# Decoding float64 weights in two VectorE steps, float16 for heads 8 to 15, and channel blocks in parts of 5, 4 and 3

## The chip, the cores and the metric

The kernel runs on one core of one Trainium2 chip. The metric is the time on the device in microseconds, median of the runs. The engines are TensorE (PE: matmuls, PEld: its weight loads), VectorE (DVE), ScalarE (ACT), GpSimd (POOL) and SyncE (SP, whose queue issues the DMAs).

## What is computed

Attention over 4 x 8 heads with a forget gate, then an MLP-mixer block, then a gated convolution block. The sequence has 576 positions, a head 64 columns, the model 512.

```python
scores = q @ k.T / 8 + (cum[:, None] - cum[None, :])   # cum = cumsum(log f), causal mask
attn = softmax(scores); x = attn @ v                    # per head; x is (4, 576, 512)
h = relu(x^T @ w_tok1) @ w_tok2;  u = x + h^T           # 576 -> 256 -> 576
y = u + relu(u @ w_ch1) @ w_ch2                         # 512 -> 1536 -> 512
h = relu(y @ w_in);  c = conv3(h, conv_w)               # 512 -> 1024
out = (h * sigmoid(c)) @ w_out                          # 1024 -> 512
```

The weights of both blocks come as float64. All else is float32.

## The kernel before

**Precision.** A float32 value is held as a high and a low float16 half, and a product is three matmuls, high x high, high x low and low x high (`mm3`, lines 262 to 267). `power_of` (232) finds a power of two from the maximum of a tensor so that the halves fit float16.

**Attention, head by head** (`pair`, `smax`, `sexp`, `pv`). Two heads' scores are made together, in three sets of blocks (lines 862 and 866). VectorE masks them and takes row maxima (880), ScalarE takes the exponential (886). Then the attention matrix is transposed. For heads under `FULL` (16 of 32) TensorE does it in float32, 13 transposes (919), and ScalarE and VectorE copy them out of PSUM (254, 932); PV is one float32 matmul per block (951), 15 blocks. Other heads, except 30 and 31, write a float16 high part on POOL (895) and a low part on VectorE (901), and two DMA transposes from SyncE turn them (911); PV is three float16 matmuls per block (956 to 958). Their V is also split into halves: a sum of absolute values (750), a scale (774), and POOL casts (257, 782). Four heads make a group; a group's token mixing follows it (lines 1059 to 1138, ordered by `group`), and two groups make a batch.

**Channel mixing.** `w_ch1` and `w_ch2` have 12 blocks of 128 hidden columns. They are split into parts (`PARTS_M`). A chunk is half a batch, 288 tokens; there are eight. For a chunk and a part `channel_mix` does 12 matmuls of 288 columns per block, a ReLU on ScalarE (534) and its remainder on VectorE (538), then 12 more per block into four outputs. The first part (`EARLY = 1`) runs beside the attention of later heads, and its results are copied (554) and stored to `p_d`; the others run after the attention and are added to `p` by VectorE (550). `gated` then does the last block, chunk by chunk.

**Weights.** `weight_set` (382) and `weight` (301) load a float64 block as pairs of 32-bit words into one of two buffers `wraw`. ScalarE scales the upper word as a float32 by 2^-112 (406, 328), which moves the exponent. VectorE shifts the result left by three and masks (410), puts the sign in (411), and puts in the top three bits of the lower word (412). A maximum (251) over each block, a spread of it over the partitions by TensorE (245) and `power_of` give the scale; ScalarE and VectorE then make the halves (442, 446). `WT` holds 15 such blocks during the attention.

**Order.** All instructions after the start are issued in an order that `Order` works out when the kernel is built, from a duration, a rank and the dependencies that each task is given (`T(...)`): per engine the task that can start first, then the one of lowest rank. Each engine then runs its list in that fixed order. `SETR` gives the ranks of the early weight sets (of `w_ch1` and of `w_ch2`), `LATER` those of the later parts.

Of the kernel before, what the change touches and what calls it, by code (L numbers as in the profile page):

```python
# [8 lines left out]
F32 = mybir.dt.float32  # L9
F32R = mybir.dt.float32r  # L10
F16 = mybir.dt.float16
I32 = mybir.dt.int32
U8 = mybir.dt.uint8
AF = mybir.ActivationFunctionType
ALU = mybir.AluOpType
# [128 lines left out]
def fox_moe_kernel(  # L144
# [14 lines left out]
    nc = tc.nc  # L159
# [14 lines left out]
    HG = 4  # L174
# [17 lines left out]
    VP_W = 130  # L192
    WSTN = 512

    PARTS_M = (3, 3, 3, 3)
    EARLY = 1
    M_AT = [sum(PARTS_M[:x]) for x in range(len(PARTS_M) + 1)]
    M1 = M_AT[EARLY]
# [2 lines left out]
    NW = 41  # L201
    MM = 0.1226

    FULL = 4 * HG
    BY_PE = [n < FULL or n >= NH - 2 for n in range(NH)]

    SETR = ((0.0, 15.0),)
    LATER = (-10.0, 10.0, 30.0)
    PER = 6.0

    const = ctx.enter_context(tc.tile_pool(name="const", bufs=1))
# [20 lines left out]
    def power_of(dst, ps, n, factor=1.0):  # L232
        nc.vector.tensor_reduce(dst[:, 1:2], ps[:, 0:n], mybir.AxisListType.X, ALU.max)
        nc.vector.tensor_scalar(dst[:, 1:2], dst[:, 1:2], 2.0 ** -60, None, ALU.max)
        up, lo = dst[:, 0:1].bitcast(I32), dst[:, 1:2].bitcast(I32)
        nc.vector.tensor_scalar(up, lo, 0x7F800000, 0x7F800000, ALU.bitwise_xor, ALU.bitwise_and)
        nc.vector.tensor_scalar(lo, lo, 0x7F800000, None, ALU.bitwise_and)
        nc.vector.tensor_scalar(dst[:, 1:2], dst[:, 1:2], 0.5 / factor, None, ALU.mult)
        if factor != 1.0:
            nc.vector.tensor_scalar(dst[:, 0:1], dst[:, 0:1], factor, None, ALU.mult)  # L240

    def spread(stat, n):
        ps = bank("w")[:, 0:128 * n]
# [39 lines left out]
    T = todo.add  # L283
# [12 lines left out]
        return bank(tag)[:, 0, :] if tag == "z" else bank(tag)  # L296


    staged = [0]

    def weight(block, place, rank, key, pools_=(), copy=None):

        src, dims = block
        p = dims[0]
        n = 1
        for d in dims[1:]:
            n *= d
        r = staged[0]
        staged[0] += 1
        box = {}  # L310
        plain = src.dtype == F32

        def shaped(ap):
            return ap.rearrange("p (k n) -> p k n", k=dims[1]) if len(dims) == 3 else ap

        def load():
            if plain:
                box["raw"] = work.tile([128, WSTN, 2], F32, tag="wraw", name="wraw", bufs=2)
                nc.sync.dma_start(shaped(box["raw"].rearrange("p n t -> p (n t)")[0:p, 0:n]), src)
                return  # L320
            box["raw"] = work.tile([128, WSTN, 2], I32, tag="wraw", name="wraw", bufs=2)
            nc.sync.dma_start(shaped(box["raw"][0:p, 0:n, :].rearrange("p n t -> p (n t)")), src.bitcast(I32))

        def exp():
            if plain:
                return
            box["t"] = (cwt if copy else WT[NE - 1 - r % 2])[0:p, 0:n]
            nc.scalar.activation(out=box["t"], in_=box["raw"][0:p, 0:n, 1].bitcast(F32), func=AF.Copy,
                                 scale=2.0 ** -112)

        def dec():
            if plain:
                box["val"] = shaped(box["raw"].rearrange("p n t -> p (n t)")[0:p, 0:n])
                return
            c = box["t"].bitcast(I32)
            nc.vector.tensor_scalar(c, c, 3, 0x7FFFFFF8, ALU.logical_shift_left, ALU.bitwise_and)
            nc.vector.scalar_tensor_tensor(c, box["raw"][0:p, 0:n, 1], -2 ** 31, c, ALU.bitwise_and, ALU.bitwise_or)
            nc.vector.scalar_tensor_tensor(c, box["raw"][0:p, 0:n, 0], 29, c, ALU.logical_shift_right,
                                           ALU.bitwise_or)
            box["val"] = shaped(c.bitcast(F32))  # L340

        def high():
            box["hi"], box["lo"] = place()
            act_cast(box["hi"], box["val"])

        def low():
            pool_sub(box["lo"], box["val"], f32(box["hi"]))

        a, c = ("wraw", r % 2), ("cwt",) if copy else ("W", NE - 1 - r % 2)
        k = n / 512.0  # L350
        T("SP", 0.4, rank - 8, load, writes=[a], moved=0.3 + 1.5 * k * p / 128)
        T("ACT", 0.15 + 0.5 * k, rank, exp, reads=[a], writes=[c])
        T("DVE", 0.2 + 2.4 * k, rank, dec, reads=[a], writes=[c])
        if copy is not None:
            T("DVE", 0.1, rank, lambda: copy(box["val"]), reads=[c], writes=[key])
            return
        T("ACT", 0.15 + 0.5 * k, rank, high, reads=[c], writes=[(key, "h")], pools=pools_)
        T("POOL", 0.1 + 1.3 * k, rank, low, reads=[c, (key, "h")], writes=[key], pools=pools_)
# [7 lines left out]
    WT = {}  # L366
# [15 lines left out]
    def weight_set(name, blocks, raws, first, ranks, cranks, factor):  # L382


        nb = len(blocks)
        stat = const.tile([128, nb], F32, name=f"stat_{name}")
        pw = power(f"pw_{name}")
        box = {}
        for k, (kind, m, (src, dims)) in enumerate(blocks):
            i = raws[k]  # L390
            r = staged[0]
            staged[0] += 1
            plain = src.dtype == F32

            def shaped(ap, dims=dims):
                return ap.rearrange("p (k n) -> p k n", k=dims[1]) if len(dims) == 3 else ap

            def load(k=k, i=i, src=src, plain=plain, shaped=shaped):
                if plain:
                    nc.sync.dma_start(shaped(WT[i]), src)  # L400
                    return
                box[k] = work.tile([128, WSTN, 2], I32, tag="wraw", name="wraw", bufs=2)
                nc.sync.dma_start(shaped(box[k].rearrange("p n t -> p (n t)")), src.bitcast(I32))

            def exp(k=k, i=i):
                nc.scalar.activation(out=WT[i], in_=box[k][:, :, 1].bitcast(F32), func=AF.Copy, scale=2.0 ** -112)

            def dec(k=k, i=i):
                c = WT[i].bitcast(I32)
                nc.vector.tensor_scalar(c, c, 3, 0x7FFFFFF8, ALU.logical_shift_left, ALU.bitwise_and)  # L410
                nc.vector.scalar_tensor_tensor(c, box[k][:, :, 1], -2 ** 31, c, ALU.bitwise_and, ALU.bitwise_or)
                nc.vector.scalar_tensor_tensor(c, box[k][:, :, 0], 29, c, ALU.logical_shift_right, ALU.bitwise_or)

            a = ("wraw", r % 2)
            w = [("W", i)]
            if plain:
                T("SP", 0.4, ranks[k] - 8, load, reads=opened(i), writes=w, moved=1.0)
            else:
                T("SP", 0.4, ranks[k] - 8, load, writes=[a], moved=1.8)
                T("ACT", 0.65, ranks[k], exp, reads=[a, *opened(i)], writes=w)  # L420
                T("DVE", 2.3, ranks[k], dec, reads=[a], writes=w)
            T("DVE", 0.65, ranks[k], lambda k=k, i=i: largest(stat[:, k:k + 1], WT[i]), reads=w,
              writes=[("stat", name, k)])

        def across():
            nc.vector.tensor_reduce(stat[:, 0:1], stat, mybir.AxisListType.X, ALU.max)

        def span():
            box["ps"] = spread(stat, 1)

        kw = turn("w")
        st = [("stat", name, k) for k in range(nb)]
        T("DVE", 0.1, cranks[0], across, reads=st[1:], writes=st[:1])
        T("PE", 0.25, cranks[0], span, reads=st, writes=[kw], ring=[kw])
        T("DVE", 0.7, cranks[0], lambda: power_of(pw, box["ps"], 128, factor), reads=[kw], writes=[("pw", name)], ring=[kw])
        for k, (kind, m, _) in enumerate(blocks):
            i = raws[k]
            j = first if k == 0 else raws[k - 1]
            wslot[kind, m] = j

            def high(i=i, j=j):
                nc.scalar.activation(out=WT[j].bitcast(F16)[:, 0:512], in_=WT[i], func=AF.Copy, scale=pw[:, 0:1])

            def low(i=i, j=j):
                t = WT[j].bitcast(F16)
                nc.vector.scalar_tensor_tensor(t[:, 512:1024], WT[i], pw[:, 0:1], t[:, 0:512], ALU.mult, ALU.subtract)

            T("ACT", 0.75, cranks[k], high, reads=[("W", i), ("pw", name), *opened(j)], writes=[("W", j)])
            T("DVE", 0.75, cranks[k], low, reads=[("W", i), ("pw", name)], writes=[("W", j)])
        return pw  # L450
# [188 lines left out]
    with tc.manual_schedule():  # L639
# [558 lines left out]
        AVAIL = [(H * (b + 1) - 1) * PER + 30 for b in range(B)]  # L1198
        LATE = 1000.0
        for k, (block, hi, lo) in enumerate(tok_w):  # L1200
            weight(block, lambda hi=hi, lo=lo: (hi, lo), 4 + 5.0 * k, ("tokw", k), pools_=["a1"])
        t0 = AVAIL[0] - 30
        at = 0
        for x in range(EARLY):
# [257 lines left out]
```

## Time and profile before

| | |
|---|---|
| median of 3 runs | 751.34 us (750.29 to 753.07) |
| the profiled execution | 751.88 us, span 750.0 us |
| TensorE busy | 732.8 us, 98% |
| VectorE busy | 563.7 us, 75% |
| ScalarE busy | 399.3 us, 53% |
| POOL busy | 182.4 us, 24% |
| mean granted clock of TensorE | 0.991 |

A busy time is the union of the engine's instructions. Matmuls overlap in the pipeline: one of 288 columns is shown with 287 ns, but the next one starts long before it ends. A float32 matmul appears as two records. In a window row, xN is the number of instructions in the window.

### The profile page before, as it was taken

To read this page: it belongs to the slowest core of one execution; us is meant where nothing else is said; L and a number is where in the kernel's file an instruction comes from. 1 tells how busy PE (TensorE), PEld (TensorE's weight loads), DVE (VectorE), ACT (ScalarE), POOL (GpSimd) and SP (SyncE) were. 2 spreads that over 40 slices of the span, in tenths; PEclk is the share of its full clock that TensorE was granted. 3 is DMA by queue.
4 is the path that set the end of the run, shared out by engine and by line. 5 is a ranking of instruction groups with operands and counts; after the bars stand their busy time and mean duration, and the time that the engine had idled before them with its cause. 6 is when DMAs were issued, how large, how long until landed. Compare 5 with 4: busy or idle time off the path is not lost.

```text
span 750.0 us, 16275 instructions
## 1 busy us (share of the span) xinstructions
PE 732.8 (98%) x6396; PEld 600.9 (80%) x6396; DVE 563.7 (75%) x1349; ACT 399.3 (53%) x862; POOL 182.4 (24%) x242
## 2 busy tenths in 40 slices
PE   7999999998999999999999999999999999999997
PEld 5889889887786878878787777778878878778785
DVE  5788899889896778878888886336749767965551
ACT  5875667665575464645324223112248766776663
POOL 2221114173646414000003103011003323323230
PEclk8999999999999999999999999999999999999999
DMA  9454544567898868835348444054111212100101
GB/s 218 148 165 154 153 137 139 185 125 192 180 230 192 162 126 280 260 106 183 128 119 244 144 142 140 2 159 126 33 64 33 64 33 64 48 18 33 34 26 38
DMA packets 126381, 94.31 MB, mean 126 GB/s; under 512 B 64672, under 2 KB 118432, under 8 KB 126304
## 3 DMA queue, kind: packets, MB, share of 16 engines
q1 hardware_dynamic: 126304, 93.27, 44.8%
q8 instruction: 50, 0.82, 0.5%
q14 instruction: 27, 0.22, 0.1%
HBM read 57.73 MB, written 23.59 MB: 108 GB/s over the span
## 4 chain that ended last, share of the span: by engine, by line
PE 81%; DVE 7%; issue 5%; POOL 3%; ACT 3%; DMA 0%; SPq 0%; POOLq 0%; ACTq 0%; DVEq 0%
PE w L265 13%; PE w L266 12%; PE w L267 12%; PE z L266 8%; PE z L265 8%; PE z L267 8%; PE w L951 7%; PE z L862 6%; PE w L919 3%; POOL g L260 2%; DVE pl L901 1%; PE w L1096 1%; PE z L866 1%; DVE t L880 1%; ACT t L886 1%
## 5 line engine op out<-in xcount | busy, mean ns | idle before, releaser
L265 PEld LDWEIGHTS <-w 128*128 128x128 f16 x1280 | 125.4, 98 | 34.5 <-issue 3.0
L267 PEld LDWEIGHTS <-w 128*128 128x128 f16 x1280 | 125.6, 98 | 33.0 <-issue 1.1
L266 PEld LDWEIGHTS <-w 128*128 128x128 f16 x1280 | 125.3, 98 | 33.2 <-issue 2.0
L534 ACT ACTIVATE r<-w 128x288 f16<-128x288 f32 x96 | 39.2, 408 | 129.8 <-PE w L267 128.7
L1362 DVE SCALAR_TENSOR_TENSOR cv<-hp,cw,cv 128x286 f32<-128x286 f32 (+1 forms) x128 | 74.7, 590 | 43.6 <-ACT cv L1356 41.4
L266 PE MATMUL w<-ul,w 128*128 128x288 f16 x352 | 101.1, 287 | 0.0
L265 PE MATMUL w<-uh,w 128*128 128x288 f16 x352 | 101.1, 287 | 0.0
L267 PE MATMUL w<-uh,w 128*128 128x288 f16 x352 | 101.0, 287 | 0.0
L260 POOL TENSOR_TENSOR g<-sg,g 128x286 f16<-128x286 f32 (+1 forms) x64 | 54.5, 858 | 168.1 <-ACT g L254 166.3
L886 ACT ACTIVATE t<-t,m 128x448 f32<-128x448 f32 (+4 forms) x160 | 81.9, 553 | 23.8 <-DVE m L880 23.2
L265 PE MATMUL z<-r,w 128*128 128x288 f16 x288 | 82.3, 286 | 0.4 <-DVE p L550 0.3
L265 PE MATMUL w<-vh,w 128*128 128x288 f16 x288 | 82.4, 286 | 0.0
L266 PE MATMUL w<-vl,w 128*128 128x288 f16 x288 | 82.4, 286 | 0.0
L267 PE MATMUL w<-vh,w 128*128 128x288 f16 x288 | 82.4, 286 | 0.0
L267 PE MATMUL z<-r,w 128*128 128x288 f16 x288 | 82.4, 286 | 0.0
L266 PE MATMUL z<-r,w 128*128 128x288 f16 x288 | 82.4, 286 | 0.0
L880 DVE CUSTOM_DVE_ANT_0 t<-z,mask 64x64 f32<-64x64 f32 (+4 forms) x160 | 70.0, 480 | 10.0 <-PE z L866 9.8
L266 PE MATMUL z<-g,w 128*128 128x286 f16 (+1 forms) x256 | 73.3, 286 | 0.7 <-POOL g L260 0.7
L265 PE MATMUL z<-g,w 128*128 128x286 f16 (+1 forms) x256 | 73.0, 285 | 1.0 <-ACT g L254 1.0
L267 PE MATMUL z<-g,w 128*128 128x286 f16 (+1 forms) x256 | 72.9, 285 | 0.0
L611 POOL TENSOR_TENSOR p<-p,u 128x288 f32<-128x288 f32 x32 | 29.1, 941 | 175.6 <-DMA p<-p_d 86.7
L550 DVE SCALAR_TENSOR_TENSOR p<-z,backs,p 128x288 f32<-128x288 f32 x96 | 48.6, 515 | 29.7 <-PE z L267 25.3
(185 smaller groups left out, 1647.0 us busy)
## 6 DMA issues: line engine op xcount, KB each, us to landing
wraw<-in_moe_w_ch_dram SPq DMA_DIRECT2D x24, 512.0 KB, 3.9
qk<-in_qk_dram SPq DMA_DIRECT2D x16, 608.0 KB, 4.9
u_d<-us SPq DMA_DIRECT2D x8, 576.0 KB, 4.3
p_d<-res SPq DMA_DIRECT2D x32, 144.0 KB, 3.1
p<-p_d SPq DMA_DIRECT2D x8, 576.0 KB, 4.6
u<-u_d SPq DMA_DIRECT2D x8, 576.0 KB, 4.5
x_d<-p SPq DMA_DIRECT2D x8, 576.0 KB, 3.2
u<-x_d SPq DMA_DIRECT2D x8, 576.0 KB, 3.9
```

Source lines behind the costliest of these rows:

```text
L260: nc.gpsimd.tensor_tensor(o, a, b, ALU.subtract)
L265: nc.tensor.matmul(ps, wh, xh, start=(first and i == 0), stop=False)
L266: nc.tensor.matmul(ps, wh, xl, start=False, stop=False)
L267: nc.tensor.matmul(ps, wl, xh, start=False, stop=(last and i == n - 1))
L534: nc.scalar.activation(out=t[:, 0, :], in_=box["z", m], func=AF.Relu)
L550: nc.vector.scalar_tensor_tensor(t, box["o", d], back, t, ALU.mult, ALU.add)
L611: nc.gpsimd.tensor_tensor(box["p"][:, d], box["p"][:, d], box["u"][:, d], ALU.add)
L862: nc.tensor.matmul(out_[x], t[r, Q0[i]:Q0[i] + 128], t[r, k0:k0 + n], start=first, stop=False)
L880: nc.vector.tensor_tensor_reduce(to, z_t.pop((n, i)), mk, -0.125, 3e38, ALU.add, ALU.min, m_t[n][0:rows, i:i + 1])
L886: nc.scalar.activation(out=tt[0:rows, o:o + w], in_=tt[0:rows, o:o + w], func=AF.Exp, bias=m_t[n][0:rows, i:i + 1], scale=-1.0)
L951: nc.tensor.matmul(o[:, 0:65], p32(n)[:, 128 * blk:128 * blk + 128], vp32_t[g % 2][:, slot, hh, :], start=(j == 0), stop=(j == nb - 1))
L1362: nc.vector.scalar_tensor_tensor(cv, hp_t[m][:, s0 + t:s1 + t], cw[:, t, m:m + 1], cv, ALU.mult, ALU.add)
```

## The change

It touches five things.

- `PARTS_M` goes from (3, 3, 3, 3) to (5, 4, 3): the early part has five blocks of twelve, and there are two later parts instead of three. `SETR` and `LATER` give other ranks, and the token weights' rank starts at 10 instead of 4.
- `FULL` goes from 16 to 8 heads: heads 8 to 15 take the float16 path, and groups 2 and 3 have their V split.
- Decoding: ScalarE uses Prelu with the slope -2^32 for negative values, so that the sign lands in a bit that survives the shift. VectorE then takes two steps, a shift of the lower word in its buffer and a shift and OR.
- The scale of a decoded block comes from ScalarE's Square with a sum (`accum_out`), written over the raw buffer, in place of VectorE's maximum. The raw buffer is thus held until Square has run. `power_of_root` makes the power of two from the sum of squares.
- The tasks' durations and dependencies follow.

```diff
-    PARTS_M = (3, 3, 3, 3)
+    PARTS_M = (5, 4, 3)
-    FULL = 4 * HG
+    FULL = 2 * HG
-    SETR = ((0.0, 15.0),)
-    LATER = (-10.0, 10.0, 30.0)
+    SETR = ((-5.0, 30.0),)
+    LATER = (-10.0, 20.0, 40.0)
+    def power_of_root(dst, ps, n, factor):
+        nc.vector.tensor_reduce(dst[:, 1:2], ps[:, 0:n], mybir.AxisListType.X, ALU.max)
+        nc.vector.tensor_scalar(dst[:, 1:2], dst[:, 1:2], 2.0 ** -120, None, ALU.max)
+        up, lo = dst[:, 0:1].bitcast(I32), dst[:, 1:2].bitcast(I32)
+        nc.vector.tensor_scalar(lo, lo, 1, 0x7F800000, ALU.logical_shift_right, ALU.bitwise_and)
+        nc.vector.tensor_scalar(up, lo, 0x7F800000, None, ALU.bitwise_xor)
+        nc.vector.tensor_scalar(dst[:, 1:2], dst[:, 1:2], 2.0 ** 64 / factor, None, ALU.mult)
+        nc.vector.tensor_scalar(dst[:, 0:1], dst[:, 0:1], 2.0 ** -65 * factor, None, ALU.mult)
+    def shifted(o, raw):
+        nc.scalar.activation(out=o, in_=raw[:, :, 1].bitcast(F32), func=AF.Prelu, scale=2.0 ** -112, alpha=-2.0 ** 32)
+    def joined(o, raw):
+        c, low = o.bitcast(I32), raw[:, :, 0]
+        nc.vector.tensor_scalar(low, low, 29, None, ALU.logical_shift_right)
+        nc.vector.scalar_tensor_tensor(c, c, 3, low, ALU.logical_shift_left, ALU.bitwise_or)
             def exp(k=k, i=i):
-                nc.scalar.activation(out=WT[i], in_=box[k][:, :, 1].bitcast(F32), func=AF.Copy, scale=2.0 ** -112)
+                shifted(WT[i], box[k])
             def dec(k=k, i=i):
-                c = WT[i].bitcast(I32)
-                nc.vector.tensor_scalar(c, c, 3, 0x7FFFFFF8, ALU.logical_shift_left, ALU.bitwise_and)
-                nc.vector.scalar_tensor_tensor(c, box[k][:, :, 1], -2 ** 31, c, ALU.bitwise_and, ALU.bitwise_or)
-                nc.vector.scalar_tensor_tensor(c, box[k][:, :, 0], 29, c, ALU.logical_shift_right, ALU.bitwise_or)
+                joined(WT[i], box[k])
+            def squares(k=k, i=i):
+                nc.scalar.activation(out=box[k][:, :, 1].bitcast(F32), in_=WT[i], func=AF.Square,
+                                     accum_out=stat[:, k:k + 1])
-                T("DVE", 2.3, ranks[k], dec, reads=[a], writes=w)
-            T("DVE", 0.65, ranks[k], lambda k=k, i=i: largest(stat[:, k:k + 1], WT[i]), reads=w,
-              writes=[("stat", name, k)])
+                T("DVE", 1.25, ranks[k], dec, reads=w, writes=[a, *w])
+            if plain:
+                T("DVE", 0.65, ranks[k], lambda k=k, i=i: largest(stat[:, k:k + 1], WT[i]), reads=w,
+                  writes=[("stat", name, k)])
+            else:
+                T("ACT", 0.9, ranks[k], squares, reads=w, writes=[a, ("stat", name, k)])
-            weight(block, lambda hi=hi, lo=lo: (hi, lo), 4 + 5.0 * k, ("tokw", k), pools_=["a1"])
+            weight(block, lambda hi=hi, lo=lo: (hi, lo), 10 + 5.0 * k, ("tokw", k), pools_=["a1"])
```

`weight` changes its decode in the same way, with a task of 0.15 + 1.2 per 512 elements in place of 0.2 + 2.4.

## Rows read from the trace of the kernel before

**Rows 1.** The page: busy time, share of the span and instructions of each engine.

```profile
PE 732.8 (98%) x6396; PEld 600.9 (80%) x6396; DVE 563.7 (75%) x1349; ACT 399.3 (53%) x862; POOL 182.4 (24%) x242
```

**Rows 2.** Busy time by stretch: from:to length, engines (instructions), granted clock, DMA share, GB/s.

```profile
10.00:50.00 40.00, 37.98 (x283) 30.95 (x285) 29.24 (x103) 32.24 (x70) 10.20 (x11) 0.93 0.56 159
50.00:90.00 40.00, 40.00 (x334) 36.00 (x335) 34.95 (x94) 25.67 (x57) 4.24 (x5) 1.00 0.55 167
90.00:163.00 73.00, 72.86 (x611) 64.78 (x609) 66.78 (x186) 46.93 (x100) 21.16 (x29) 1.00 0.54 157
163.00:286.00 123.00, 116.49 (x1417) 96.17 (x1414) 102.69 (x282) 73.20 (x155) 56.57 (x57) 0.97 0.78 173
...
375.00:400.00 25.00, 25.00 (x206) 20.03 (x205) 21.50 (x59) 8.15 (x18) 0.00 (x0) 1.00 0.59 144
```

**Rows 3.** Waits of TensorE, 90 to 286 us: total, times, longest in us.

```profile
PE w L245 <- DVE um L251: 2.8, 1, 2.8
```

**Rows 4.** The chain that ended last, in order of time: start, us, what.

```profile
20.17 3.49 PE w L951 x30
...
69.84 1.32 PE w L919 x12
```

**Rows 5.** Timeline: first PV matmul of head 27, and the next other one.

```profile
261.62 0.19 PE L956 MATMUL w<-vp,pt 128*128 128x65 f16 x1
...
263.01 0.28 PE L265 MATMUL w<-r,w 128*128 128x288 f16 x1
```

**Rows 6.** Groups by line and shape: busy us, mean ns, idle time before.

```profile
L550 DVE SCALAR_TENSOR_TENSOR p<-z,backs,p 128x288 f32<-128x288 f32 x96 | 48.6, 515 | 29.7 <-PE z L267 25.3 <-issue 4.0
L538 DVE SCALAR_TENSOR_TENSOR r<-w,r 128x288 f16<-128x288 f32 x96 | 43.4, 453 | 35.2 <-ACT r L534 34.4
...
L411 DVE SCALAR_TENSOR_TENSOR w<-wraw,w 128x512 int32<-128x512 int32 x40 | 30.6, 765 | 1.4
...
L406 ACT ACTIVATE w<-wraw 128x512 f32<-128x512 f32 x40 | 26.7, 672 | 16.2 <-DMA wraw<-in_moe_w_in_dram 6.5 <-DMA wraw<-in_moe_w_out_dram 5.3 <-DMA wraw<-in_moe_w_ch_dram 4.3
...
L901 DVE SCALAR_TENSOR_TENSOR pl<-t,ph 128x1024 f16<-128x1024 f32 x14 | 19.7, 1404 | 1.3 <-POOL ph L895 1.3
L446 DVE SCALAR_TENSOR_TENSOR w<-w,pw_c,w 128x512 f16<-128x512 f32 x24 | 19.1, 794 | 3.0 <-ACT w L442 3.0
...
L410 DVE TENSOR_SCALAR w<-w 128x512 int32<-128x512 int32 x40 | 18.8, 471 | 2.8 <-ACT w L406 2.7
...
L251 DVE TENSOR_REDUCE stat_c<-w 128x1 f32<-128x512 f32 x24 | 16.2, 674 | 0.1
...
L901 DVE SCALAR_TENSOR_TENSOR pl<-t,ph 128x640 f16<-128x640 f32 x14 | 13.8, 983 | 1.9 <-POOL ph L895 1.8
...
L932 DVE COPY pt<-w 128x512 f32<-128x512 f32 x16 | 10.9, 682 | 2.1 <-PE w L919 2.0
```

**Rows 7.** Groups of ScalarE, same columns: load of the table for Exp, accumulator read.

```profile
L886 ACT ACT_TABLE_LOAD x1 | 1.3, 1283 | 0.0
...
L750 ACT ACTIVATION_READ_ACCUMULATOR junk<-vf 128x1 f32 x4 | 0.8, 189 | 0.0
```

**Rows 8.** DMA issues, of a block of weights: KB each, median us to landing.

```profile
wraw<-in_moe_w_ch_dram SPq DMA_DIRECT2D x24, 512.0 KB, 3.9
```

**Rows 9.** The last decoding step (line 412) by stretch: VectorE busy (instructions), clock, DMA.

```profile
50.00:90.00 40.00, 5.93 (x7) 1.00 0.55 167
90.00:163.00 73.00, 5.56 (x7) 1.00 0.54 157
163.00:286.00 123.00, 0.00 (x0) 0.97 0.78 173
```

**Rows 10.** ReLUs (line 534), then result copies (554), of the mix in heads 16 to 31.

```profile
163.00:286.00 123.00, 4.04 (x10) 0.97 0.78 173
...
163.00:286.00 123.00, 5.93 (x12) 0.97 0.78 173
```

**Rows 11.** All ReLUs of the mix (line 534): ns min/median/max, first and last start.

```profile
L534 ACT ACTIVATE r<-w x96: 387/410/411, 119.4 to 550.9; 128x288 f16<-128x288 f32 x96
```

More of the change, by code (lines that the diff above doesn't have):

```diff
@@ L327, in exp @@
             box["t"] = (cwt if copy else WT[NE - 1 - r % 2])[0:p, 0:n]
-            nc.scalar.activation(out=box["t"], in_=box["raw"][0:p, 0:n, 1].bitcast(F32), func=AF.Copy,
-                                 scale=2.0 ** -112)
+            shifted(box["t"], box["raw"][0:p, 0:n])
         def dec():
@@ L334, in dec @@
                 return
-            c = box["t"].bitcast(I32)
-            nc.vector.tensor_scalar(c, c, 3, 0x7FFFFFF8, ALU.logical_shift_left, ALU.bitwise_and)
[L337 to L340, printed above, removed]
+            joined(box["t"], box["raw"][0:p, 0:n])
+            box["val"] = shaped(box["t"])
         def high():
@@ L352, in weight @@
         T("ACT", 0.15 + 0.5 * k, rank, exp, reads=[a], writes=[c])
-        T("DVE", 0.2 + 2.4 * k, rank, dec, reads=[a], writes=[c])
+        T("DVE", 0.15 + 1.2 * k, rank, dec, reads=[c], writes=[a, c])
         if copy is not None:
@@ L388, in weight_set @@
         box = {}
+        bring = power_of if blocks[0][2][0].dtype == F32 else power_of_root
+        if bring is power_of_root:
+            factor *= 4.0
         for k, (kind, m, (src, dims)) in enumerate(blocks):
@@ L405, in exp @@
             def exp(k=k, i=i):
-                nc.scalar.activation(out=WT[i], in_=box[k][:, :, 1].bitcast(F32), func=AF.Copy, scale=2.0 ** -112)
+                shifted(WT[i], box[k])
             def dec(k=k, i=i):
-                c = WT[i].bitcast(I32)
-                nc.vector.tensor_scalar(c, c, 3, 0x7FFFFFF8, ALU.logical_shift_left, ALU.bitwise_and)
-                nc.vector.scalar_tensor_tensor(c, box[k][:, :, 1], -2 ** 31, c, ALU.bitwise_and, ALU.bitwise_or)
-                nc.vector.scalar_tensor_tensor(c, box[k][:, :, 0], 29, c, ALU.logical_shift_right, ALU.bitwise_or)
+                joined(WT[i], box[k])
+            def squares(k=k, i=i):
+                nc.scalar.activation(out=box[k][:, :, 1].bitcast(F32), in_=WT[i], func=AF.Square,
+                                     accum_out=stat[:, k:k + 1])
             a = ("wraw", r % 2)
@@ L434, in weight_set @@
         T("PE", 0.25, cranks[0], span, reads=st, writes=[kw], ring=[kw])
-        T("DVE", 0.7, cranks[0], lambda: power_of(pw, box["ps"], 128, factor), reads=[kw], writes=[("pw", name)], ring=[kw])
+        T("DVE", 0.7, cranks[0], lambda: bring(pw, box["ps"], 128, factor), reads=[kw], writes=[("pw", name)], ring=[kw])
         for k, (kind, m, _) in enumerate(blocks):
```

## The prediction

> **What bounds the kernel now.** I read four views in this order: the page's busy times, the busy time by stretch, the chain that ended last, and the groups by line. The page gives TensorE 98% of the span and VectorE 75% [rows 1]. Busy time of TensorE overlaps, so I check it by counting: in 375 to 400 us it runs 206 matmuls of 288 columns, one each 0.121 us, with no gap [rows 2]. From 310 us on the kernel is that: a queue of channel-mix and output matmuls. Time comes off there only if matmuls go away.
>
> Before 310 us there are three stages. In 10 to 50 us TensorE is idle 2.0 us of 40 by the busy row. In 50 to 163 us (heads 4 to 15) it is idle 0.1 us; here the float32 attention keeps it full, and VectorE is nearly full as well (66.8 of 73 us in 90 to 163) [rows 2]. In 163 to 286 us (heads 16 to 31, float16) TensorE is idle 6.5 us of 123, and its mean granted clock is 0.97 there against 1.00 before, 3% of 123 us, 3.7 us lost [rows 2]. So float16 heads cost 10.2 us of idle and slow time over 16 heads, 0.64 us each; float32 heads cost next to none. One idle stretch there is a wait for VectorE: 2.8 us in a spread of the group's maximum [rows 3].
>
> The profiled execution took 751.88 us with a span of 750.0; the median is 751.34. I sum against 751.9 and take 0.5 off at the end.
>
> **Heads 8 to 15 in float16 (TensorE).** A float32 head does its PV in 30 recorded matmuls, 3.49 us, and 13 transposes at 1.32/12 = 0.11 us, 1.43 us [rows 4]. A float16 head does 45 matmuls for PV: head 27 begins at 261.62 and the next matmul begins at 263.01, so 1.39 us [rows 5], and its transposes go to the DMA. Saved per head: 3.49 + 1.43 - 1.39 = 3.53 us. The chain's 3.49 includes the tail of the last matmul (some 0.13 us of issue), so I take 3.41; eight heads, 27.3 us (28.2 at most). This is TensorE work, in a stage where TensorE had no gap, so it is worth its full size if something fills TensorE afterwards. Two more value sums for groups 2 and 3 cost it under 1 us, and two weight sets less give that back.
>
> **Parts 5, 4, 3.** No matmul is added or removed: two more of twelve blocks for eight chunks, 2 x 24 x 8 = 384 matmuls, 46.5 us at 0.121, move from the late to the early queue. Early ones are what fills TensorE beside the heads. 32 additions on VectorE (one part less, 8 chunks, 4 each, 0.515 us) go away, 16.5 us; they lay beside a TensorE that starts a matmul each 0.121 us, so I cost them at nothing; if VectorE set the pace there they would be worth up to that.
>
> **The decode.** Per weight VectorE ran 471 ns, twice 765 (line 412 is of the same form as 411) and a maximum of 674 [rows 6]. Now it runs one single-source step and one of 0.765. The single-source step reads every second word; its bounds are L410's 471 ns (also single-source, contiguous) and L411's 765 (the same strided buffer, but two sources). I take 471, the row with the same form. So 0.765 + 0.674 = 1.44 us less per weight, 1.14 at least. For the 26 weights decoded after 163 us that is 37 us, again beside a full TensorE: nothing, by the same reason and with the same price if the cover went. The Trainium skill, "VectorE: DVE Perf Modes", section "What auto-detection actually checks", asks unit steps only of 16-bit tensors for a doubled rate, so it would keep the strided step near 0.47; no row of this trace shows a strided single-source step.
>
> ScalarE gets Prelu for Copy at equal size (672 ns for 512 elements) and a Square with an accumulator: I price it as one more such pass plus the accumulator read of 189 ns, 0.86 us [rows 6, 7], at least 0.67. ScalarE is busy 46.9 of 73 us in 90 to 163 [rows 2], so ten of them, 8.6 us, hide in the 26 that are free; without that cover they would cost those 8.6. Square is a new wait of ScalarE for VectorE: the Exps of the next blocks and the evacuations of PSUM queue behind it, and VectorE and TensorE wait for those. What waits behind them: the raw buffer is released by Square instead of by the decode. One turn of a buffer was 3.9 us landing [rows 8] + 0.67 + 2.00 = 6.6 us; it becomes 3.9 + 0.67 + 1.24 + 0.86 = 6.7. The load that queues on SyncE behind it is therefore not later.
>
> **VectorE while heads 8 to 15 run.** Start from 66.8 us [rows 2]. The low parts cost 1.404 + 0.983 and replace a copy of 0.682, eight times: +13.6. Seven decodes fall there [rows 9]: -10.0 (-7.9 at the slow bound). Five low halves more at 0.79: +4.0. Ten remainders of the early mix, one batch, at 0.453: +4.5 [rows 6]. Sum 78.9. TensorE has 73 - 27.3 = 45.7 us of attention there, and one batch of early mix (240 x 0.121 = 29.0): 74.7. So VectorE becomes the longer one: 4.2 us of TensorE idle if VectorE were full, 11.5 if it stays at its present share (78.9/0.915 = 86.2). The 0.64 us per head of the existing float16 heads gives 5.1 for eight. I take 6.5, nearest to that row since it is the same work, and keep 4 and 11.5.
>
> POOL gets eight heads' high parts and the values of two groups; it is busy 21.2 of 73 us there, and 56.6 of 123 where nearly every head has them. SyncE gets sixteen transposes; the DMA share is 0.54 in that stage and 0.78 where nearly every head has them [rows 2]. Neither is last.
>
> **Sum.** 751.9 - 27.3 + 6.5 = 731.1; less 0.5, 730.6. I forecast **731 us**.
>
> **The rivals.** *VectorE relief removes old idle too.* The 10.2 us of idle and slow time in 163 to 286 are queue order and VectorE lateness; more early mix lies ready there (batches 0 and 1 together 58 us; now 10 ReLUs and 12 result copies run there, 10 x 12 + 12 x 9 = 228 matmuls, 28 us [rows 10]), and lighter decoding also helps the start, 2 us idle. If half to all of it went, 5 to 12 us: 719 to 726. Against it: hardly any decode runs in 163 to 286 (none of the third steps [rows 9]), so the relief is elsewhere.
>
> *The fill is smaller than the hole.* VectorE at its present share (11.5), plus a clock of 0.97 over that stage too and two to three waits like the 2.8 us one: idle 13 to 22, so 738 to 747. For it: VectorE at 66.8 of 73 already.
>
> *The gain is eaten.* Idle of 24 to 31: 748 to 755. It needs the same loss in heads 16 to 31 as well.
>
> *The early mix comes too late, slower.* This is the other side. The second half of a mix needs all ten early weights, where six sufficed, and the new ranks put its five weights at 30, behind heads of lower rank. Before, the first ReLU of the early mix ran at 119.4 us [rows 11]. Fourteen weights were decoded by 163 us, seven before 90 [rows 9]; at that pace the tenth is decoded near 121 us and its halves are done near 130, while the first halves can start earlier. If instead the set is ready only after head 15, TensorE has 45.7 us of work in a stage that VectorE paces at 79 to 86: idle 33 to 40, 751.4 - 27.3 + 33..40 = 757 to 764. It turns slower than now beyond 0.5% when idle passes 31 us, that is when fewer than (86 - 45.7 - 31)/0.121, some 75, early-mix matmuls run before head 16.
>
> *Prelu or Square isn't in the table loaded with Exp.* Then a decode between two Exps costs two loads of 1.283 us [rows 7]; 21 decodes in 10 to 163 us make 54 us on a ScalarE that is busy 104.8 of 153 there [rows 2], and with the Squares it would need some 171: 18 us beyond the stage and more in waits, 745 to 765. Against it: Copy, Abs, Relu and Exp alternate now, with one load at the first Exp [rows 7]. The Trainium skill, "ScalarE: Activation LUTs", section "Table sets: the hidden batching unit", names relu, copy, identity and abs as members of every set, and does not name Prelu or Square there; with its figure of about 2.66 us for a switch the 54 us would be an estimated 112.
>
> **How the numbers follow.** About 0.5% (747.6 to 755.1) is what a measurement of this kernel can tell from no change. Forecast, 726 to 738: 0.53. VectorE relief, 717 to 726: 0.21. Smaller fill, 738 to 747: 0.15. Eaten: 0.05. Early mix too late: 0.04. Table loads: 0.02. Faster 0.89, same 0.05, slower 0.06. The range 717 to 745 leaves out the last three and the upper end of the third.
>
> **What would show it.** The PV of heads 8 to 15 at 1.39 us each and only 130 recorded transposes (10 heads); early mix running beside heads 8 to 15; the attention ending near 310 us still, but with far more early mix done by then; seven of twelve blocks left for after it; the saturated stage at 0.121 us as now. The strided step at 0.47 or 0.77 us. One Exp table load. I am wrong if TensorE idles over 20 us more before 310, or if the float16 heads' stage is longer than 86 us for eight heads.

## The result, and the profile after

| | before | after |
|---|---|---|
| median | 751.49 us (750.29 to 753.07, 4 runs) | 728.29 us (725.97 to 730.78, 4 runs) |
| ratio of the medians | | 0.9691 [0.9653, 0.9729] |
| the profiled execution | 751.88 us, span 750.0 | 727.58 us, span 725.8 |
| PE, DVE, ACT, POOL busy | [rows 1] | 706.5, 502.8, 420.8, 214.8 us |

The forecast was 731 us with a range of 717 to 745. Line numbers moved, by 11 in the helpers (`mm3` 276, spread of a maximum 256, maximum 262) and by 23 behind the decoding: scores 885, masks 903, Exp 909, high parts 918, low parts 924, transposes 942, float32 PV 974, float16 PV 979 to 981, early ReLU 557, early copies 577, low halves 469.

Busy time by stretch of the changed kernel, columns as in [rows 2]:

```profile
10.00:50.00 40.00, 38.83 (x296) 32.36 (x298) 25.16 (x94) 31.70 (x71) 10.68 (x15) 0.91 0.60 173
50.00:90.00 40.00, 37.77 (x305) 33.12 (x302) 31.08 (x89) 29.54 (x65) 17.63 (x21) 0.98 0.55 158
90.00:163.00 73.00, 67.34 (x729) 53.58 (x728) 68.92 (x176) 50.48 (x108) 39.78 (x34) 0.94 0.91 204
163.00:286.00 123.00, 121.22 (x1433) 99.98 (x1430) 100.38 (x273) 73.18 (x154) 57.41 (x56) 1.00 0.93 200
...
375.00:400.00 25.00, 25.00 (x206) 20.02 (x205) 18.29 (x48) 14.28 (x33) 0.00 (x0) 1.00 0.46 124
```

Against [rows 2], two stages changed in opposite directions. In 50 to 163 us TensorE was idle for 0.1 us only and had its full clock; now it is idle 2.23 + 5.66 us at a clock of 0.98 and 0.94. In 163 to 286 it was idle 6.5 us at 0.97; now 1.8 at 1.00. The saturated queue at 375 us runs 206 matmuls in 25 us, as before.

Groups by line and shape of the changed kernel: busy us, mean ns of one, idle before.

```profile
L318 DVE SCALAR_TENSOR_TENSOR w<-w,wraw 128x512 int32<-128x512 int32 x42 | 32.5, 773 | 8.1 <-ACT w L313 4.8
...
L313 ACT ACTIVATE w<-wraw 128x512 f32<-128x512 f32 x42 | 27.9, 672 | 4.1 <-DMA wraw<-in_moe_w_out_dram 2.1 <-DMA wraw<-in_moe_w_in_dram 1.3 <-DMA wraw<-in_moe_w_ch_dram 0.6
...
L431 ACT ACTIVATE wraw<-w 128x512 f32<-128x512 f32 x40 | 26.9, 673 | 19.4 <-DVE w L318 18.2 <-DVE rs L989 1.0
...
L317 DVE TENSOR_SCALAR wraw<-wraw 128x512 int32<-128x512 int32 x42 | 20.3, 483 | 1.6 <-DMA wraw<-in_moe_w_in_dram 1.2 <-DMA wraw<-in_moe_w_ch_dram 0.3
...
L942 PE MATMUL w<-ident,t 128*128 128x128 f32 x130 | 17.9, 278 | 0.6 <-DVE pt L963 0.2 <-ACT t L909 0.2 <-DVE xf L998 0.2
...
L431 ACT ACTIVATION_READ_ACCUMULATOR wraw<-w 128x1 f32 x40 | 7.4, 186 | 0.0
...
L909 ACT ACT_TABLE_LOAD x1 | 1.3, 1283 | 0.0
```

The decode is two VectorE steps of 483 and 773 ns, Square costs 0.673 + 0.186 = 0.86 us, 130 transposes are left (10 heads of 13), and the table for Exp is loaded once. The timeline shows the first two of the new float16 heads, the first PV matmul and the first one after them; 2.76 us for both, 1.38 us a head:

```profile
99.66 0.20 PE L979 MATMUL w<-vp,pt 128*128 128x65 f16 x1
...
102.42 0.46 PE L256 MATMUL w<-ident,um 128*128 128x128 f32 x2
```

TensorE's waits of the changed kernel over the whole execution (total, times, longest in us). The wait for the group's maximum is down from 2.8 [rows 3] to 0.8, and those for a mask lead:

```profile
PE z L885 <- DVE m L903: 3.9, 4, 1.8
...
PE w L256 <- DVE um L262: 0.8, 1, 0.8
```

**A balance from the window rows.** Take as time lost by TensorE in a stretch its idle time plus (1 - granted clock) x length, as the prediction did for heads 16 to 31. Then a kernel's span should be 750.0, less the 27.3 us of TensorE work where heads 8 to 15 are float16, plus the difference in lost time. For the thirteen other kernels (below) this gives the measured span within 4.1 us, and for the changed one 727.6 against 725.8. "Chain" is the time that VectorE's decoding steps hold on the chain that ended last (with the old decode the maximum of each block too), added up over its pieces from 10 to 310 us. All times in us, from the profiled execution.

| kernel | span | lost 10-50 | 50-163 | 163-286 | 286-330 | sum | span worked out | chain |
|---|---|---|---|---|---|---|---|---|
| before | 750.0 | 4.8 | 0.1 | 10.2 | 0.0 | 15.1 | | 0 |
| after | 725.8 | 4.8 | 13.1 | 1.8 | 0.4 | 20.0 | 727.6 | 1.7 |
| f16_only | 753.1 | 3.6 | 14.2 | 21.2 | 2.6 | 41.6 | 749.2 | 19.7 |
| decode_only | 754.8 | 5.0 | 2.1 | 12.4 | 0.7 | 20.2 | 755.1 | 5.2 |
| parts_only | 762.1 | 12.7 | 5.2 | 5.3 | 0.4 | 23.6 | 758.5 | 12.0 |
| no_f16 | 741.6 | 5.0 | 0.2 | 3.7 | 0.0 | 8.9 | 743.8 | 0 |
| no_decode | 760.3 | 9.5 | 20.6 | 18.2 | 0.4 | 48.7 | 756.3 | 20.6 |
| no_parts | 749.3 | 4.8 | 16.3 | 16.0 | 5.2 | 42.3 | 749.9 | 7.5 |
| no_join | 726.7 | 4.7 | 14.4 | 1.8 | 0.4 | 21.3 | 728.9 | 0 |
| v_late | 739.1 | 4.4 | 21.0 | 9.6 | 0.4 | 35.4 | 743.0 | 4.0 |
| tok_rank4 | 727.7 | 4.8 | 13.5 | 1.8 | 0.9 | 21.0 | 728.6 | 9.0 |
| true_costs | 738.0 | 2.8 | 18.1 | 9.4 | 0.4 | 30.7 | 738.3 | 2.5 |
| parts66 | 730.9 | 4.6 | 16.7 | 0.1 | 0.6 | 22.0 | 729.6 | 5.5 |
| full12 | 729.1 | 4.0 | 2.7 | 0.6 | 0.7 | 8.0 | 729.3 | 3.0 |

(full12 has half of the 27.3 us. Fixed windows hold slightly different heads in each kernel, and what is lost after 330 us is not in the table. The idle times that some expectations name, 68 and 38 us, 30 us added, 18 us before head 16, are larger than its figures, 41.6, 15.1, 26.5 and 13.1. tok_rank4 is as fast as the changed kernel with 9.0 us of decoding on its chain against 1.7, so time on the chain is not a price by itself.)

### The profile page after: what moved, and what is told of

Read it like the earlier page. It is cut to its first block, busy times and chain, and to the rows that moved or that the text cites. A ratio compares the mean times of both kernels' runs of the same rounds, so it can differ in the third digit from the quotient of the medians.

```text
span 725.8 us, 16282 instructions
## 1 busy us (share of the span) xinstructions
PE 706.5 (97%) x6412; PEld 573.8 (79%) x6412; DVE 502.8 (69%) x1225; ACT 420.8 (58%) x924; POOL 214.8 (30%) x270
## 4 chain that ended last, share of the span: by engine, by line
PE 81%; DVE 7%; issue 6%; POOL 4%; ACT 1%; DMA 0%; SPq 0%; POOLq 0%; DVEq 0%; ACTq 0%
PE w L276 14%; PE w L277 14%; PE w L278 14%; PE z L277 7%; PE z L278 7%; PE z L276 7%; PE z L885 6%; PE w L974 3%; PE w L942 2%; POOL g L271 2%; PE z L889 2%; DVE pl L924 1%; PE w L1119 1%; PE w L980 1%; PE w L979 1%
## 5 line engine op out<-in xcount | busy, mean ns | idle before, releaser
L276 PE MATMUL w<-uh,w 128*128 128x288 f16 x416 | 119.8, 288 | 0.0
L278 PE MATMUL w<-uh,w 128*128 128x288 f16 x416 | 119.6, 288 | 0.0
L277 PE MATMUL w<-ul,w 128*128 128x288 f16 x416 | 119.6, 288 | 0.0
L909 ACT ACTIVATE t<-t,m 128x576 f32<-128x576 f32 (+4 forms) x160 | 81.7, 554 | 20.9 <-DVE m L903 18.5
L903 DVE CUSTOM_DVE_ANT_0 t<-z,mask 128x576 f32<-128x576 f32 (+4 forms) x160 | 70.5, 479 | 17.9 <-PE z L889 17.8
L561 DVE SCALAR_TENSOR_TENSOR r<-w,r 128x288 f16<-128x288 f32 x96 | 43.4, 453 | 43.4 <-ACT r L557 43.2
L885 PE MATMUL z<-qk 64*128 64x288 f32 (+4 forms) x384 | 61.8, 432 | 7.0 <-DVE m L903 3.9
L271 POOL TENSOR_TENSOR xl<-xf,xh 128x320 fp32r<-128x320 f32 x32 | 34.0, 1064 | 110.2 <-ACT xh L265 110.1
L276 PE MATMUL w<-vh,w 128*128 128x288 f16 x224 | 64.1, 286 | 0.0
L277 PE MATMUL w<-vl,w 128*128 128x288 f16 x224 | 64.1, 286 | 0.0
L278 PE MATMUL w<-vh,w 128*128 128x288 f16 x224 | 64.1, 286 | 0.0
L276 PE MATMUL z<-r,w 128*128 128x288 f16 x224 | 64.1, 286 | 0.0
```

Of the source, the lines that this page charges most:

```text
L271: nc.gpsimd.tensor_tensor(o, a, b, ALU.subtract)
L276: nc.tensor.matmul(ps, wh, xh, start=(first and i == 0), stop=False)
L277: nc.tensor.matmul(ps, wh, xl, start=False, stop=False)
L278: nc.tensor.matmul(ps, wl, xh, start=False, stop=(last and i == n - 1))
L561: nc.vector.scalar_tensor_tensor(t[:, 1, :], box["z", m], 0.0, f32(t[:, 0, :]), ALU.max, ALU.subtract)
L885: nc.tensor.matmul(out_[x], t[r, Q0[i]:Q0[i] + 128], t[r, k0:k0 + n], start=first, stop=False)
```

## The experiments

The theories on record: in one (A) the lighter decode on VectorE is what keeps TensorE fed beside the float16 heads; in the other (B) it is the larger early part, with its new ranks. Each of the first six kernels has one or two of the three parts of the change.

**Float16 for heads 8 to 15 alone** (from the kernel before).

```diff
-    FULL = 4 * HG
+    FULL = 2 * HG
```

> The kernel before with only heads 8 to 15 in float16; old decode, parts of 3. If the gain is TensorE work taken away (27.3 us), most of it comes here, less idle: VectorE then has 66.8 + 13.6 = 80.4 us to do beside heads 8 to 15, and TensorE 45.7 us of attention plus 17.4 of early mix, so 17 to 25 us of idle: 741 to 750. If the gain is VectorE's relief by the decode, this is no faster than before: 751 or more. If it is the moved mix, the same.

755.68 us, 1.0064 [1.0045, 1.0084]. The first range is missed: slightly slower than before, the outcome named for a gain by the decode or by the moved mix. TensorE's 27.3 us went, and 26.5 us came back as lost time, 14 in heads 4 to 15 and 11 in heads 16 to 31; another 3.0 us are idle in 330 to 500 us. Heads 16 to 31 of this kernel:

```profile
163.00:286.00 123.00, 109.14 (x1210) 87.75 (x1209) 111.31 (x287) 71.25 (x147) 57.38 (x53) 0.94 0.90 201
```

VectorE is busy 111.3 of 123 us and TensorE idles 13.9. The chain that ended last says with what (start, us, what; L410 to L412 are the old decode, L880 the mask):

```profile
163.66 1.17 DVE w L410
...
164.86 1.03 DVE w L411
...
165.91 2.44 DVE w L412
168.36 0.40 DVE t L880
...
168.81 0.91 ACT t L886 x2
```

One decode holds VectorE for 4.7 us between two masks, and the mask and the Exp wait for it. TensorE has other work until 180 us (no idle time in 160 to 180); then it is idle 3.4 and 3.1 us in the next two stretches of 10 us, waiting for low halves of `u` and for masks, VectorE's work. By the groups' means the decode should take 2.0 us [rows 6]. Its last step took 2.44 us where the median of line 412 in this kernel is 0.692. POOL's timeline in that stretch, and that of the kernel before:

```profile
164.62 3.20 POOL L782 TENSOR_TENSOR vp<-vf,vp 64x256 f16<-64x256 f32 x2
...
165.07 3.86 POOL L782 TENSOR_TENSOR vp<-vf,vp 64x256 f16<-64x256 f32 x3
```

POOL is doing the value split of a later group, and it did the same at that time in the kernel before; the splits of the two added groups ran at 51 and 91 us. What is new beside it is the decode. Line 412 in heads 16 to 31 of this kernel, where the kernel before ran none [rows 9]:

```profile
163.00:286.00 123.00, 7.01 (x6) 0.94 0.90 201
```

Before, fourteen ran in 50 to 163 us; here eight do, and six come later, among VectorE's 111.3 us of work. In all the old decode holds 19.7 us of this kernel's chain, and 0 of the kernel before's.

**The decode alone** (`shifted`, `joined`, Square, `power_of_root` and their tasks; `FULL`, `PARTS_M` and ranks as before).

```diff
-                T("DVE", 2.3, ranks[k], dec, reads=[a], writes=w)
+                T("DVE", 1.25, ranks[k], dec, reads=w, writes=[a, *w])
...
+                T("ACT", 0.9, ranks[k], squares, reads=w, writes=[a, ("stat", name, k)])
```

> The kernel before with only the new decode and the sums of squares. If TensorE's work sets the time, the relief can only remove idle that VectorE causes in heads 16 to 31 and at the start: 746 to 751. If VectorE's relief is the gain: 728 to 738.

756.78 us, 1.0075 [1.0051, 1.0098]. A miss, slightly slower. There is little to gain where TensorE hardly waited: lost time is 20.2 against 15.1, 2.0 more in 50 to 163 us and 2.2 more in heads 16 to 31.

**The parts and ranks alone.**

```diff
-    PARTS_M = (3, 3, 3, 3)
+    PARTS_M = (5, 4, 3)
-    SETR = ((0.0, 15.0),)
-    LATER = (-10.0, 10.0, 30.0)
+    SETR = ((-5.0, 30.0),)
+    LATER = (-10.0, 20.0, 40.0)
```

(and the token weights' rank 10 for 4)

> The kernel before with only parts of 5, 4, 3 and their ranks. TensorE's work is unchanged and it is full beside heads 4 to 15; more early mix can only fill the idle of heads 16 to 31: 747 to 753 if TensorE's work sets the time. If moving the mix is the gain: 730 to 740.

764.29 us, 1.0185 [1.0148, 1.0221]. A miss, and the slowest. Heads 16 to 31 did gain (10.2 lost to 5.3: 14 ReLUs of the mix run there, against 10 in [rows 10]). Most of the loss is at the start, 12.7 for 4.8; 5.1 more are lost in 50 to 163, and TensorE is idle 3.8 us in 330 to 400. The chain at 33 us, where lines 336 to 338 are the old decode in `weight`:

```profile
32.96 0.63 DVE w L336
...
33.62 0.47 DVE w L337
...
34.11 0.44 DVE w L338
...
35.24 0.23 DVE w L336
...
36.92 0.67 DVE t L880
```

Two decodes stand ahead of a mask (the new decode with the same ranks, no_f16, loses 5.0 in this stage), and after the gap TensorE runs at a lower clock, in 30 to 50 us:

```profile
30.00:40.00 10.00, 7.99 (x53) 5.80 (x52) 8.11 (x25) 7.99 (x17) 3.99 (x4) 0.86 0.33 98
40.00:50.00 10.00, 8.95 (x51) 8.15 (x50) 6.66 (x23) 6.38 (x13) 0.80 (x1) 0.63 0.35 116
```

51 matmul records in the second 10 us, where the kernel before starts 82.

**The change without float16 for heads 8 to 15.**

```diff
-    FULL = 2 * HG
+    FULL = 4 * HG
```

> The kernel after with heads 8 to 15 back in float32; new decode, parts of 5, 4, 3. If the gain is the 27.3 us of TensorE work, it is nearly all gone: 743 to 751. If it is decode and parts together: 728 to 738.

743.57 us, 0.9897 [0.9873, 0.9922], at the lower end of the first range. Decode and parts together gain 7.9 us where each alone loses. Lost time in heads 16 to 31 falls from 10.2 to 3.7. From here to the changed kernel the work falls by 27.3 and the lost time rises by 11.1: 16.2 us, measured 15.8 in the spans.

**The change with the old decode.**

```diff
-                joined(WT[i], box[k])
+                c = WT[i].bitcast(I32)
+                nc.vector.tensor_scalar(c, c, 3, 0x7FFFFFF8, ALU.logical_shift_left, ALU.bitwise_and)
+                nc.vector.scalar_tensor_tensor(c, box[k][:, :, 1], -2 ** 31, c, ALU.bitwise_and, ALU.bitwise_or)
+                nc.vector.scalar_tensor_tensor(c, box[k][:, :, 0], 29, c, ALU.logical_shift_right, ALU.bitwise_or)
```

(and the maximum for Square)

> The kernel after with the old three-step decode and VectorE's maximum. In the single-part runs TensorE's work came out as counted (27 us less with float16 heads, unchanged else) and all the rest of the time was idle between matmuls. Theory A, idle is VectorE's load beside the heads, and the decode pays it: the idle of float16 alone (68 us against 38 before) stays or grows, as the early mix adds VectorE work: 748 to 762. Theory B, the early mix alone fills the holes and the decode is beside it: 728 to 738.

762.24 us, 1.0139 [1.0119, 1.016]. It is A's outcome, just past its upper end: lost time is 48.7 where float16 alone had 41.6. Without the new decode the change is slower than the kernel before by 10.8 us; with it, faster by 23.2. The old steps hold 20.6 us of the chain, the new ones 1.7. Lost time is higher in every stage up to 286 us, and TensorE, which the changed kernel keeps busy for all 70 us of 330 to 400, waits there for two maxima and a copy of `conv_w` and has a lower clock after it:

```profile
330.00:400.00 70.00, 65.97 (x534) 52.67 (x533) 57.63 (x130) 35.06 (x69) 0.13 (x2) 1.00 0.53 160
400.00:500.00 100.00, 99.99 (x803) 79.43 (x804) 65.58 (x139) 30.24 (x60) 13.09 (x16) 0.98 0.46 139
```

The early mix comes later too: 9 of its ReLUs run in heads 16 to 31, 12 in the changed kernel (below).

**The change with the old parts and ranks.**

```diff
-    PARTS_M = (5, 4, 3)
+    PARTS_M = (3, 3, 3, 3)
```

(and `SETR`, `LATER` and the token weights' rank as before)

> The kernel after with parts of 3, 3, 3, 3 and the old ranks. Theory A: with the decode's relief, 10 us and more of the 30 us of added idle go: 735 to 746. Theory B, no gain without more early mix: 750 to 757, as with float16 alone.

748.41 us, 0.9953 [0.9936, 0.997], between the two theories. So both count. What the parts give lies in heads 16 to 31 and just after, 16.0 + 5.2 lost against 1.8 + 0.4, and hardly before head 16 (16.3 against 13.1). The profiled execution, 751.08 us, lies 2.7 us over its median, so some of the loss is that execution's. Heads 16 to 31:

```profile
163.00:286.00 123.00, 110.68 (x1308) 90.50 (x1305) 105.31 (x285) 74.50 (x154) 61.92 (x58) 0.97 0.98 203
```

ScalarE's ReLUs (line 557) and copies (line 577) of the early mix in heads 16 to 31 of the changed kernel:

```profile
163.00:286.00 123.00, 4.86 (x12) 1.00 0.93 200
...
163.00:286.00 123.00, 6.96 (x14) 1.00 0.93 200
```

A ReLU stands for 12 matmuls and a copy now for 15 (five blocks of three): 12 x 12 + 14 x 15 = 354 early matmuls there, where [rows 10] gave 228. At 0.121 us that is 43 us of filling instead of 28.

**What is the lighter decode worth once its order stands?** The changed kernel, same order, but VectorE's two decode steps are left out of `weight_set`.

```diff
             def dec(k=k, i=i):
-                joined(WT[i], box[k])
+                pass
```

> The kernel after, in the same order, with the two decoding steps of VectorE left out for the channel and output weights (they are then not decoded): some 15 blocks x 1.26 us = 19 us less VectorE work before 182 us, where TensorE was idle 18 us between 50 us and head 16. If VectorE's load makes that idle, 8 to 15 us of it go: 713 to 721. If the chains of the heads (score, exponential, transposes by DMA) and the order make it: 725 to 730.

728.42 us, 0.97 [0.9675, 0.9726]: as the changed kernel.

```profile
50.00:90.00 40.00, 37.77 (x304) 33.12 (x301) 25.22 (x79) 29.35 (x64) 16.23 (x21) 0.98 0.55 156
90.00:163.00 73.00, 67.51 (x716) 53.83 (x716) 61.71 (x162) 49.57 (x105) 34.58 (x34) 0.92 0.85 196
```

VectorE does 13 us less in these two stretches and TensorE is as busy as before, 37.77 and 67.51 against 37.77 and 67.34. So it is not VectorE's total load that leaves TensorE idle in the changed kernel. The chain into its worst gap, in the changed kernel and then in no_join:

```profile
93.96 2.40 POOL vp L805
96.37 1.46 POOL ph L918
...
98.43 2.26 POOL ph L918
...
100.71 1.65 DVE pl L924
102.36 1.26 DVE um L262
...
105.47 0.50 DVE xf L998 x2
...
106.19 0.35 DVE t L903
...
106.60 1.33 PE z L885 x4
```

```profile
93.29 2.55 DVE w L469
...
99.54 1.83 POOL ph L918
...
106.86 0.35 DVE t L903
```

In the changed kernel it is POOL's value split of group 3, then the high parts of the next heads, then on VectorE a low part, the maximum for a group's token mix and its scales, all ahead of the mask that TensorE's scores wait for. No decode is among them. In no_join the low half of a weight, which ran beside that split, stands on the chain in its place; from the high parts on the chain is the same, and the gap is no shorter. TensorE's stretches of the changed kernel there and what followed:

```profile
100.00:110.00 10.00, 7.46 (x105) 5.58 (x102) 9.17 (x19) 6.21 (x11) 4.97 (x5) 0.78 0.96 223
110.00:120.00 10.00, 9.88 (x103) 7.15 (x101) 9.21 (x23) 4.80 (x13) 1.45 (x2) 0.88 1.05 213
```

**Can the gap be closed by order?** Three kernels move or re-time what stands in it. First, the value split of groups 3 and later three heads later:

```diff
-                v_tasks(g + 1, (HG * g + 2) * PER)
+                v_tasks(g + 1, (HG * g + 2 + (3 if g >= 2 else 0)) * PER)
```

> The kernel after with the split of V of groups 3 and later ranked three heads later, so that POOL does the high parts of heads 9 and 10 first. In the trace of after, POOL casts group 3's V from 89.9 to 96.4 us while the high parts of head 9 or 10 wait, and TensorE is idle some 9 us in 100 to 125. If POOL's order makes that hole: 720 to 726. If VectorE's load makes it: 727 to 730.

740.84 us, 0.9848 [0.9827, 0.9869]: both expectations missed. The high part of head 10 began at 95.3 us in place of 96.3, since it waits for its scores and Exp and not for POOL alone, while the order around it shifted and head 8's PV moved to 114 us. 21.0 us are lost in 50 to 163.

Second, the token weights' rank back at 4:

```diff
-            weight(block, lambda hi=hi, lo=lo: (hi, lo), 10 + 5.0 * k, ("tokw", k), pools_=["a1"])
+            weight(block, lambda hi=hi, lo=lo: (hi, lo), 4 + 5.0 * k, ("tokw", k), pools_=["a1"])
```

> The kernel after with the token weights' rank back at 4 instead of 10: no work changes, only the order. If the interaction of the parts is real and the order's own scatter is small: 725 to 733. If a small change of order alone moves it by 5 us or more, the differences between the single parts are largely the order's scatter: outside of 723 to 734.

728.89 us, 0.9696 [0.9679, 0.9712]: no difference.

Third, the order planned with durations nearer to the trace:

```diff
-            T("DVE", 0.75, cranks[k], low, reads=[("W", i), ("pw", name)], writes=[("W", j)])
+            T("DVE", 0.95, cranks[k], low, reads=[("W", i), ("pw", name)], writes=[("W", j)])
```

(and high parts 1.35 and 1.0 for 1.15 and 0.8, low parts 1.4 and 1.0, `x_lo` 1.05, halves of `u` 0.97)

> The kernel after with its order built from durations nearer to those measured (high parts 1.35 and 1.0, low parts 1.4 and 1.0, low halves of weights 0.95, of u 0.97, remainders of x 1.05). No work changes. If the idle beside the float16 heads comes from an order that was planned with too short durations: 715 to 725. If the order is good enough, only scatter: 724 to 740, as a later V has shown 12 us on its own.

740.73 us, 0.9868 [0.9838, 0.9897], slower by 12 us, in both stages, and just past the second range. Truer durations alone don't make a better order.

**How much early mix, how many float32 heads?** Two parts of six blocks:

```diff
-    PARTS_M = (5, 4, 3)
+    PARTS_M = (6, 6)
-    LATER = (-10.0, 20.0, 40.0)
+    LATER = (-10.0,)
```

> The kernel after with parts of 6 and 6. TensorE's work is the same. Heads 16 to 31 have only 4 us of idle left, and the hole at heads 8 to 11 lies before the first early mix, so more early mix has little to fill: 725 to 731. If the amount of early mix still limits it: 715 to 723.

736.24 us, 0.9801 [0.9764, 0.9838], slower than with 5, 4, 3, and past both ranges. Heads 16 to 31 are full (0.1 us lost), but 16.7 are lost in heads 4 to 15: more early mix serves only where it is ready. The profiled execution, 732.65 us, lies 3.6 us under its median, so some of the loss isn't in the table.

Twelve float32 heads:

```diff
-    FULL = 2 * HG
+    FULL = 3 * HG
```

> The kernel after with heads 8 to 11 back in float32, 12 to 15 in float16. TensorE's work grows by half of 27.3, 13.6 us. If the hole lies where the float16 heads begin before the early mix is ready, most of the 18 us of idle from 50 us to head 16 goes with it: 726 to 733. If the idle belongs to every float16 head, half of it goes: 733 to 738.

731.41 us, 0.9742 [0.9708, 0.9776], as expected. Four heads give back half of the work saved, 13.65 us, and 12.0 us of lost time go, 10.4 of them in 50 to 163. So the gap belongs to heads 8 to 11, where the early mix isn't ready (first ReLU at 112.4 us in the changed kernel) and float32 PV would cover the chain. Float16 there gains next to nothing, 1.7 us by this balance and 3.1 by the medians.

No variant beats the changed kernel.

## Why the prediction was right, and where its steps were not

**TensorE's saving: right.** PV takes 1.38 us a head in place of 3.49 [rows 4], eight heads' 104 transposes are gone, and with 27.3 us the balance closes to 4.1 us in every kernel that has the eight float16 heads.

**The idle of heads 8 to 15: mis-sized.** I took 6.5 us and 11.5 as the end; in 50 to 163 us there are 7.9 idle and 5.2 of lower clock, 13.0 more than before, the lower end of the rival "the fill is smaller". Two things failed. The range came from VectorE's share, and no_join shows that this isn't what sets it. What the runs show in its place is a chain through POOL and VectorE at the worst gap, and that the loss belongs to heads 8 to 11 (full12), with the early mix starting at about 109 us. Whether another order would shorten that chain stays open; the three tried did not. And the granted clock, which I had counted in the old float16 stage, I left to a rival here. "Neither is last" was wrong for POOL: it is on the chain before the worst gap. The DMA share went to 0.91, and a weight block now lands in 5.0 us and not 3.9 [rows 8], so that a turn of the raw buffer is 5.0 + 0.67 + 1.26 + 0.86 = 7.8 us and not 6.7; none of TensorE's waits names a weight's load.

```profile
wraw<-in_moe_w_ch_dram SPq DMA_DIRECT2D x24, 512.0 KB, 5.0
```

The stage lasts 82.5 us for eight heads (PV of head 8 at 99.7, of head 16 at 182.2 us), in the 79 to 86 forecast.

**The idle of heads 16 to 31: assumed unchanged, and 8.4 us of its 10.2 went.** That is the rival "relief", held at 0.21. My argument against it was that hardly any decode runs there; but the 43 us of early mix for 28 fill it, as parts_only shows alone (5.3 lost) and no_parts from the other side (16.0). Beside the float16 heads it takes the new decode too: no_decode has the same parts and loses 18.2 there. The two misses nearly cancel: +13.0 - 8.4 + 0.4 = 5.0 us, with nothing from the start, where the sum had 6.5. That the total came so close is luck.

**The decode at nothing: wrong.** I counted 10 us of its relief in VectorE's sum for heads 8 to 15, and priced the rest, after 163 us, at nothing. That holds while TensorE has float32 work to cover it (decode_only gains nothing). I priced the cover as staying. The float16 heads take it away, and the change with the old decode takes 34 us more (762.24 against 728.29). By stages it is 4.7 us of lost time in 10 to 50, 7.5 in 50 to 163, 16.4 in 163 to 286, and 6.0 in 330 to 500 (4.0 idle and 2.0 of lower clock), where the prediction had TensorE full: 34.6, and the spans differ by 34.5. How much of it is the steps' run time and how much the order made from their planned durations (2.3 us for a decode, now 1.25) wasn't tried; no_join shows only that below the new decode's load there is nothing more to get in this order.

**The parts at nothing: half right.** That the 32 additions less gave nothing isn't contradicted: the balance, which doesn't know of them, is 1.8 us over the measured span with them gone and 0.6 over it in no_parts, and a gap of that size is within its error of 4 us. But as filling the parts are worth 22 us of lost time (3.2 + 14.2 + 4.8 by stages, no_parts against the changed kernel), 20 us by the medians. Like the decode's 34, that holds with the order made for each kernel.

**The early mix too late: not so.** Its first ReLU (ns min/median/max, first and last start) ran at 112.4 us, before at 119.4 [rows 11], and nine ran by 163 us where I had counted ten:

```profile
L557 ACT ACTIVATE r<-w x96: 386/410/417, 112.4 to 526.7; 128x288 f16<-128x288 f32 x96
```

**Prices.** The strided step took 483 ns (taken 471; the other bound was 765), Square 0.86 us (0.86), the table one load. The Trainium skill, "VectorE: DVE Perf Modes", section "What auto-detection actually checks", which asks unit steps only of 16-bit tensors, agrees with the 483 ns.

**What one part is worth has no answer here.** By medians: float16 alone +4.2 us, decode +5.3, parts +12.8; float16 and decode -3.1, decode and parts -7.9, float16 and parts +10.8; all three -23.2. Changes of order that mean nothing by themselves (v_late, true_costs) move 12 us, so single figures of that size are partly the scatter of the order. The 34 us of the decode and the 20 of the parts are above it.

## What to carry to other kernels

Work that is hidden is hidden by something: when a change removes the cover, price again all that lay under it. The chain names what to suspect; a kernel without the step says what it is worth. Make the balance by stage (work, idle, granted clock) from start to end; to 330 us it closed to about 4 us for all kernels here, and it showed two errors that the total hid. Try parts of a change in pairs as well as alone.

## What was unexpected of the hardware

VectorE's steps are longer beside POOL's work. Line 412 has a median of 0.692 us and took 2.44 beside POOL's value split (above); the joining step of the changed kernel (line 318) has the same median and a longest of 1.40. Of its 42 on 512 elements, the 31 with no POOL instruction beside them took 0.691 to 0.696 us, the 11 with one up to 1.40, half of them over 1.0. The strided single-source step (line 317) shows it as well: 31 took 0.387 to 0.445 us, 11 beside POOL up to 1.225. So a group's mean belongs to the POOL work that ran beside it: the low halves of the early weights rose from 794 to 970 ns with POOL at 39.8 us for 21.2 in 90 to 163.

```profile
L469 DVE SCALAR_TENSOR_TENSOR w<-w,pw_c,w 128x512 f16<-128x512 f32 x24 | 23.3, 970 | 2.6 <-ACT w L465 2.6
```

The other way round, POOL's value split before the worst gap took 4.30 us in the changed kernel and 3.52 in no_join; other VectorE work shifted there too, so that POOL is held up by VectorE is likely and not shown.

The Trainium skill, "SBUF — State Buffer", section "Who interferes with whom", says that a VectorE instruction with two inputs in SBUF contends with a GpSimd instruction that reads it. The rows of lines 412 and 318 agree; I hadn't weighed that rule.

Twice the clock is low after a gap and comes back late. In the changed kernel TensorE idles 2.5 us in 100 to 110, and a chain of early-mix matmuls of 288 columns then starts one each 0.24 us, the 1.2 GHz level, until 112.4 us, and each 0.12 us after that:

```profile
112.12 0.24 PE w L278
112.36 0.20 PE w L276
112.56 0.12 PE w L277
```

In parts_only the clock of 40 to 50 us is 0.63 after 2.0 us of idle in 30 to 40 (both rows above): (1 - 0.63) x 10 = 3.7 us on top of the idle time.
